# Gated attention and a maxout layer on one core: which output products are made of seven half products, and where five loads of v stand

## The chip, the core and the metric

The kernel runs on one core of one Trainium2 chip. The metric is the time of one execution in microseconds of the device; several executions are timed and the median is taken. A profile is one execution of its own, recorded by the hardware profiler.

## The reference

Eight sequences of 3072 tokens pass through an attention without softmax, gated by u, and then through a maxout layer with an output product.

```python
# u, v: (8, 3072, 256); z: (8, 3072, 64)
scores = (1.0 / S) * np.matmul(z, z.transpose(0, 2, 1))
attn = np.maximum(scores, 0.0) ** 2
x = u * np.matmul(attn, v)               # (24576, 256) in rows
# w1, w2: (256, 1024); w_out: (1024, 256)
g = np.maximum(x @ w1, x @ w2)
out = g @ w_out
```

The kernel computes max(x w1, x w2) as relu(x (w1 - w2)) + x w2, so that the output is g w_out + x (w2 w_out), where g now means the rectified part.

## The kernel before, in words

The work is cut into 48 steps: a step n is one group s of 512 tokens (n = 6 b + s, s from 0 to 5) of one sequence b. In its step each group gets its attention products with all 24 blocks of 128 keys. Scores between two groups are made once: the tile of a group and a later one is rectified, squared, and also transposed by a DMA on SP's queue (the tiles named aT), so that the later step can read it.

The attention product of a step (`add_sums`, line 613) is itself a Strassen-like product in the form of Winograd with seven half products: VectorE makes sums of tiles (es) and of v (lf, `add_fold`, line 366), TensorE makes the products X and Y into the two accumulator banks acc, and `add_ends` (line 750) puts them together: a copy e by ScalarE, sums by VectorE, and a multiplication with the transposed u that gives xT.

Three steps later on TensorE the second layer follows (`add_second`, line 1065): four products of xT with w1 - w2 (the pieces "da" and "db"), each rectified into g, and then the output product of g with w_out plus xT with W2o. The output product of step n stands at the beginning of step n + 3 (`put_o`, line 1276). It has two forms:

- The plain form (`parts`, line 1184): for four blocks of 128 tokens, ten products each with 256 moving columns, as two halves of 64 rows that run side by side, 80 matmuls in all. Two pairs of PSUM banks hold the result, and ScalarE (or VectorE) copies each pair out (`oc`).
- Seven half products (`add_seven`, line 924): g and w_out are cut into quarters, VectorE makes four sums of quarters of g (G1 to G4, tiles gs and g_sb), TensorE makes 72 matmuls of 128 rows and 128 moving columns, ScalarE copies twice (oc0, oc1), and VectorE adds the pieces into the output tile o_sb in six sums (oA to oF).

Which form a step takes is set in line 241: by s in `SEVEN` (line 54) and n below 46. Before the change that is s = 0, 1, 2 and 4, 31 steps in all.

Halves of 64 rows that write the same bank are ordered by a mark: a one-column memset on POOL that waits for the newest matmul (`mark`, line 94), and for which a later matmul waits. POOL also issues the loads of u, v and z (`load`, line 107); such a load waits for the newest matmul at its place in TensorE's order. So a load can stand ahead of a mark in POOL's queue. `quiet` (line 1477) moves a load's place to the next job of a list of jobs (`QUIET`, line 1473) behind which no mark is due soon. `at_step(b, s, us)` names the job of TensorE that by the plan's costs begins so many microseconds after step s of sequence b.

The tiles of v for a sequence are six loads of 512 tokens, in the order of `v_order` (line 319): groups 1, 2, 3, 4, 5, 0 for every sequence but the first. Two loads share a tile, and six such tiles exist (line 65): two sequences' worth. The sums lf of a pair can begin when both its loads have landed.

TensorE's order is written out by the planner from the list of jobs. The order on VectorE, ScalarE, SP and POOL comes from a list scheduler with costs and due times (`find_orders`, line 1748), which also chooses the engine of rectifiers and squares (lines 1787 and 1793); it is run 24 times, and the best plan is kept. Both change when the costs of jobs or the places of loads change.

Of the kernel before, what the change touches and what calls it, by code (L numbers as in the profile page):

```python
# [11 lines left out]
def kernel(  # L12
# [38 lines left out]
    NDIAG = 2  # L51
    PLAIN = 3
    NA, NT, WIDE = 16, 18, 19
    SEVEN = (0, 1, 2, 4)
    SEVEN_FROM, SEVEN_TO = 0, 46
    SPARE_D = (46, 2)
    DIAG_LAG = 8700, 6700
# [49 lines left out]
    def load(timed=False, **kw):  # L107
        dma = pin(nc.gpsimd.dma_start(**kw))
        if timed:
            tc.add_manual_dep(  # L110
                dma.ins,
                newest[0].name,
                mybir.DependencyInfo(mybir.DependencyClass.Sync, mybir.DependencyReason.DATA),
                reason="timed load",
            )
# [108 lines left out]
    def job(key, ways, fn, deps=(), new=None, uses=(), after=(), lag=100):  # L224
        assert key not in jobs, key
        jobs[key] = Job(key, ways, fn, deps, new, uses, after, lag)

    def buf(pool, key, make):
        bufs[pool, key] = Buf(make)
        order.setdefault(pool, []).append(key)  # L230
# [4 lines left out]
    class Step:  # L235
        def __init__(self, n, b, s):
# [3 lines left out]
            self.parted = 0 < n < B * NG - LAG + 1  # L240
            self.seven = s in SEVEN and SEVEN_FROM <= n < SEVEN_TO
            self.count = [0] * KD
# [76 lines left out]
    def v_order(b):  # L319
        return [1, 2, 3, 4, 5, 0] if b else list(range(NG))  # L320

    def v_pair(b, g):

        return divmod(v_order(b).index(g), 2)

    def v_key(b, g):
        return ("v", (b, v_pair(b, g)[0]))

    def v_tile(b, g):
        return tile_of(*v_key(b, g))[:, v_pair(b, g)[1]]  # L330
# [13 lines left out]
    def add_v(b, g, at):  # L344
        first = v_pair(b, g)[1] == 0
        if first:
            buf(*v_key(b, g), lambda: vpool.tile([P, 2, G, D], bf16, name="v_sb"))

        def fetch(_):
            load(  # L350
                timed=at is not None,
                out=v_tile(b, g),
                in_=v[b].rearrange("(p t) d -> p t d", p=P)[:, ds(g * G, G), :],
            )

        job(
            ("v", b, g),
            {"POOL": 1300},
            fetch,
            new=v_key(b, g) if first else None,  # L360
            uses=[v_key(b, g)],
            after=list(at or ()) + ([] if first else [("v", b, v_order(b)[v_order(b).index(g) - 1])]),
            lag=8000,
        )
# [1099 lines left out]
    def pe_job_at(ns):  # L1464
        found = [key for key, at in zip(pe_order, pe_at) if at >= ns]
        return [found[0]] if found else [pe_order[-1]]


    def at_step(b, s, us):
        return pe_job_at(starts[NG * b + s] + us * 1000)  # L1470
# [6 lines left out]
    def quiet(at):  # L1477
        i = pe_order.index(at[0])
        if pe_at[i] < starts[LAG]:
            return at  # L1480
        found = [key for key in pe_order[i:] if key in QUIET]
        return found[:1] or at
# [32 lines left out]
    def add_z(b, at, turn_at):  # L1515
        def fetch(_):
            load(
                timed=True,
                out=z_sb_0[:, 1 : 1 + NSB, :],
                in_=z[b].rearrange("(p t) d -> p t d", p=P),  # L1520
            )

        def turn_z(_):
            seqs[b].zT = make_zT(z_sb_0)

        job(("z", b), {"POOL": 1800}, fetch, after=at, lag=7500)
        job(("zT", b), {"SP": 3500}, turn_z, deps=[("z", b)], after=turn_at, lag=3500)
# [3 lines left out]
    for n in range(len(steps)):  # L1531
        b, s = steps[n].b, steps[n].s
# [5 lines left out]
    for b in range(1, B):  # L1538
        if b == 1:
            z_at, zT_at = (2, 6), (3, 2)  # L1540
            v_at = [(0, 8), (3, 12), (3, 16), (4, 4), (4, 8), (5, 4)]
        else:
            z_at, zT_at = (2, 9), (3, 4)
            v_at = [(3, 11), (3, 16), (4, 5), (4, 12), (5, 2), (5, 6)]
        add_z(b, quiet(at_step(b - 1, *z_at)), at_step(b - 1, *zT_at))
        for g, at in zip(v_order(b), v_at):
            add_v(b, g, quiet(at_step(b - 1, *at)))

    W2, W2T = ("T", "w2"), ("T", "w2T")
    bufs[W2] = Buf(lambda tag: widepool.tile([P, KD, Dff], bf16, name="w2_sb", tag=tag))  # L1550
# [421 lines left out]
```

## Time and profile before

| What | Value |
|---|---|
| timed runs | 907.89, 915.62 and 908.76 us; median 908.76 |
| the profiled execution | 907.76 us |
| its span | 905.9 us |
| TensorE (PE) | 898.3 us busy, 13565 matmuls |
| weight loads (PEld) | 673.1 us |
| VectorE (DVE) | 811.1 us |
| ScalarE (ACT) | 687.6 us |
| GpSimd (POOL) | 89.0 us |
| granted clock of TensorE | 1.00 |

The span runs from the first to the last instruction of the program; the time of the execution holds a little more at both ends. Busy times are unions of an engine's instructions. Matmuls are pipelined, so that one of 256 columns is shown with 0.27 us while the next starts after 0.11; times of products are therefore taken here from start to start.

Durations that the prediction uses, as mean time of one instruction from the groups of the profile:

| Instruction | Count | Mean |
|---|---|---|
| DVE gs<-g_sb, 128x1024 | 62 | 689 ns |
| DVE gs<-g_sb,gs, 128x1024 | 31 | 688 ns |
| DVE g_sb<-g_sb, 128x1024 | 31 | 690 ns |
| DVE o_sb<-o_sb,s_ps, 128x256 | 93 | 417 ns |
| DVE ot<-o_sb,s_ps, 128x256 | 31 | 416 ns |
| DVE o_sb<-o_sb,s_ps, 128x512 | 31 | 681 ns |
| DVE o_sb<-o_sb,ot, 128x512 | 31 | 683 ns |
| DVE a_sb<-a_sb (a square), 128x1024 | 160 | 689 ns |
| DVE a_sb<-a_sb (a square), 128x256 | 8 | 284 ns |
| ACT a_sb<-a_sb (a square), 128x1024 | 133 | 1068 ns |
| ACT a_sb<-a_sb (a square), 128x256 | 37 | 435 ns |
| ACT o_sb<-s_ps, 128x512 | 63 | 593 ns |
| ACT o_sb<-s_ps, 128x256 | 35 | 376 ns |
| POOL load of v | 48 | 534 ns |
| POOL mark | 302 | 102 ns |
| from a load's issue to its landing | 48 | 5.3 us (median) |

### The profile page before, as it was taken

The numbers are of one execution on the slowest core, as the hardware profiler recorded it, in microseconds if no ns is written. First come the engines' busy times: TensorE is split into PE (matmuls) and PEld (weight loads), VectorE is DVE, ScalarE is ACT, GpSimd is POOL, SyncE is SP. The second block draws the span as 40 slices with busy tenths as digits, with TensorE's granted clock in tenths as the row PEclk, the third lists the DMA queues.
The fourth block names the chain that finished last, engine by engine and source line by source line (L and its number), as shares of the span: only waits on it lengthen the run. The fifth ranks groups of instructions, "written<-read, shape, count | busy, mean of one in ns | idle before, by whom it ended". The sixth has DMA issues, their size and how long they took to land.

```text
span 905.9 us, 31722 instructions
## 1 busy us (share of the span) xinstructions
PE 898.3 (99%) x13565; PEld 673.1 (74%) x13565; DVE 811.1 (90%) x1594; ACT 687.6 (76%) x852; POOL 89.0 (10%) x417
## 2 busy tenths in 40 slices
PE   9999999999999999999999999999999999999998
PEld 3367777777777877778777877778777777777785
DVE  6888999899998999899998999989999899998970
ACT  8867987678877788677896688965989569885625
POOL 3101000111011110001100011000200011000000
PEclk9999999999999999999999999999999999999999
DMA  9999999999999999999999999999899989997711
GB/s 158 182 182 187 195 181 132 195 135 167 188 144 193 158 150 169 175 182 167 147 165 192 173 154 143 176 196 162 145 171 161 200 139 166 177 151 149 123 60 72
DMA packets 382911, 146.32 MB, mean 162 GB/s; under 512 B 361264, under 2 KB 362928, under 8 KB 382768
## 3 DMA queue, kind: packets, MB, share of 16 engines
q1 hardware_dynamic: 366208, 114.54, 74.4%
q0 software_dynamic: 16560, 29.74, 22.5%
q8 instruction: 106, 1.74, 0.8%
q14 instruction: 37, 0.30, 0.1%
HBM read 59.77 MB, written 25.17 MB: 94 GB/s over the span
## 4 chain that ended last, share of the span: by engine, by line
PE 94%; ACT 2%; DVE 2%; issue 1%; DMA 0%; POOL 0%; POOLq 0%; DVEq 0%
PE acc L87 48%; PE s_ps L87 46%; ACT a_sb L276 1%; DVE es L290 1%; ACT a_held L276 0%; ACT a_sb L282 0%; DVE es L293 0%; DVE o_sb L290 0%; DMA o_sb<-in_z_dram 0%; ACT o_sb L287 0%; DVE e L290 0%; DVE aT L293 0%; DVE xT L297 0%; DVE ot L290 0%; DVE a_sb L293 0%
## 5 line engine op out<-in xcount | busy, mean ns | idle before, releaser
L87 PEld LDWEIGHTS <-v_sb 64*128 64x128 bf16 (+1 forms) x4464 | 311.4, 94 | 80.1 <-POOL mark_sb L95 14.5
L276 ACT ACTIVATE a_sb<-s_ps 128x1024 bf16<-128x1024 f32 x337 | 300.7, 946 | 88.5 <-PE s_ps L87 87.3
L87 PEld LDWEIGHTS <-lf 64*128 64x128 bf16 x3240 | 251.4, 94 | 44.8 <-POOL mark_sb L95 15.5
L87 PE MATMUL acc<-es,v_sb 64*128 64x256 bf16 x2160 | 277.9, 269 | 0.4 <-DVE es L290 0.4
L87 PE MATMUL acc<-es,lf 64*128 64x256 bf16 x1080 | 247.8, 269 | 0.1
L87 PE MATMUL acc<-a_sb,lf 64*128 64x256 bf16 x1224 | 226.9, 269 | 0.0
L276 ACT ACTIVATE g_sb<-s_ps 128x1024 bf16<-128x1024 f32 x187 | 186.0, 1028 | 9.7 <-PE s_ps L87 8.4
L87 PE MATMUL s_ps<-xT,w_sb 64*128 64x512 bf16 (+1 forms) x1484 | 189.4, 377 | 1.2 <-ACT g_sb L276 0.9
L87 PE MATMUL acc<-aT,lf 64*128 64x256 bf16 x936 | 174.3, 269 | 0.0
L282 ACT ACTIVATE a_sb<-a_sb 128x1024 bf16<-128x1024 bf16 (+1 forms) x170 | 153.1, 930 | 0.8
L87 PE MATMUL acc<-a_sb,v_sb 64*128 64x256 bf16 (+1 forms) x1352 | 140.8, 280 | 0.1
L284 DVE TENSOR_TENSOR a_sb<-a_sb 128x1024 bf16<-128x1024 bf16 (+1 forms) x168 | 111.0, 669 | 29.4 <-ACT a_sb L276 27.9
L290 DVE TENSOR_TENSOR e<-e,acc 128x512 f32<-128x512 f32 (+1 forms) x225 | 125.8, 576 | 9.3 <-PE acc L87 5.2
L87 PEld LDWEIGHTS <-w_sb 64*128 64x128 bf16 (+1 forms) x1488 | 69.1, 94 | 72.1 <-POOL mark_sb L95 29.7
L87 PEld LDWEIGHTS <-g_sb 64*128 64x128 bf16 (+1 forms) x2016 | 107.8, 96 | 13.0 <-issue 7.0
L87 PE MATMUL s_ps<-zT 64*128 64x512 bf16 (+2 forms) x774 | 115.6, 333 | 0.5 <-DVE zT L131 0.3
L290 DVE TENSOR_TENSOR es<-aT 128x1536 bf16<-128x1536 bf16 (+1 forms) x117 | 105.9, 931 | 0.9 <-PE acc L87 0.2
L287 ACT COPY o_sb<-s_ps 128x256 f32<-128x256 f32 (+1 forms) x98 | 47.1, 516 | 72.7 <-PE s_ps L87 72.7
L95 POOL MEMSET mark_sb<- 128x1 bf16 x302 | 30.7, 102 | 719.3 <-PE acc L87 477.2
L87 PE MATMUL s_ps<-w_out_sb,g_sb 64*128 64x256 bf16 (+1 forms) x1520 | 99.4, 253 | 0.0
L87 PE MATMUL acc<-aT,v_sb 64*128 64x256 bf16 x936 | 84.8, 270 | 0.1
L293 DVE TENSOR_TENSOR es<-a_sb 128x512 bf16<-128x512 bf16 x198 | 79.9, 418 | 3.8 <-PE acc L87 3.3
(68 smaller groups left out, 878.8 us busy)
## 6 DMA issues: line engine op xcount, KB each, us to landing
out_dram<-o_sb SPq DMA_DIRECT2D x47, 512.0 KB, 5.3
v_sb<-in_v_dram POOLq DMA_DIRECT2D x48, 256.0 KB, 5.3
u_sb<-in_u_dram POOLq DMA_DIRECT2D x48, 256.0 KB, 5.1
aT<-a_sb SPq DMA_TRANSPOSE x230, 4.4
z_sb<-in_z_dram POOLq DMA_DIRECT2D x7, 384.0 KB, 7.2
w_sb<-in_moe_w_dram POOLq DMA_DIRECT2D x2, 512.0 KB, 7.3
uT<-u_sb SPq DMA_TRANSPOSE x48, 4.7
a_sb<-a_sb SPq DMA_TRANSPOSE x45, 4.4
```

What stands on the lines that cost most here:

```text
L87: newest[0] = pin(nc.tensor.matmul(*args, **kw)).ins
L95: ins = pin(nc.gpsimd.memset(mark_sb, 0.0)).ins
L276: pin(nc.scalar.activation(out_ap, in_ap, AF.Relu))
L282: pin(nc.scalar.activation(ap, ap, AF.Square))
L284: pin(nc.vector.tensor_mul(ap, ap, ap))
L287: pin(nc.scalar.copy(out_ap, in_ap) if eng == "ACT" else nc.vector.tensor_copy(out_ap, in_ap))
L290: pin(nc.vector.tensor_add(*args))
L293: pin(nc.vector.tensor_sub(*args))
```

## The change

Two things are edited. The set of steps whose output is made of seven half products loses s = 4: steps 4, 10, 16, 22, 28, 34 and 40 take the plain form (step 46 took it already), which leaves 24 steps of 31. And the six loads of v of the second sequence (b = 1) get other places, of which the first is the same; they are no longer moved by `quiet`. Loads of later sequences keep their rule.

```diff
-    SEVEN = (0, 1, 2, 4)
+    SEVEN = (0, 1, 2)
     SEVEN_FROM, SEVEN_TO = 0, 46
...
         if b == 1:
             z_at, zT_at = (2, 6), (3, 2)
-            v_at = [(0, 8), (3, 12), (3, 16), (4, 4), (4, 8), (5, 4)]
+            v_at = [(0, 8), (3, 9), (3, 14), (4, 2), (5, 2), (5, 8)]
...
         for g, at in zip(v_order(b), v_at):
-            add_v(b, g, quiet(at_step(b - 1, *at)))
+            add_v(b, g, quiet(at_step(b - 1, *at)) if b > 1 else at_step(b - 1, *at))
```

In the built program TensorE's order is the same job for job; 7 x 72 matmuls of 128 rows become 7 x 80 of 64 rows. VectorE has 1548 instructions instead of 1596: 70 of the seven steps are gone, and 22 squares (15 of 128x1024, 7 of 128x256) have come over from ScalarE. ScalarE has 22 fewer: those squares, while two copies for each of the seven steps stay, as two of 128x512 in place of one of 128x256 and one of 128x512. POOL has 14 more marks. The loads of v wait for other matmuls, and the order of squares, sums, transposes and stores in the first sequence is rearranged; the store of step 2, for one, stands ten places later on SP's queue.

## Prediction

> **What bounds the kernel now.** I read four views, from the whole to the place. First the page's busy times with its chain of work, and TensorE's own waits:
>
> ```profile
> span 905.9 us, 31722 instructions
> ...
> PE 898.3 (99%) x13565; PEld 673.1 (74%) x13565; DVE 811.1 (90%) x1594; ACT 687.6 (76%) x852; POOL 89.0 (10%) x417
> ...
> PE 94%; ACT 2%; DVE 2%; issue 1%; DMA 0%; POOL 0%; POOLq 0%; DVEq 0%
> ```
>
> ```profile
> PE s_ps L87 <- ACT g_sb L276: 0.9, 1, 0.9
> PE acc L87 <- DVE es L290: 0.4, 1, 0.4
> PE s_ps L87 <- POOL mark_sb L95: 0.3, 1, 0.3
> ```
>
> TensorE is the bound: 99% busy, 94% of the chain. Its waits after the start are three, 1.6 us together. The windows say where:
>
> ```profile
> 80.00:100.00 20.00, 19.47 (x304) 14.74 (x300) 18.84 (x41) 17.92 (x24) 2.19 (x9) 1.00 1.09 191
> 100.00:120.00 20.00, 18.94 (x290) 14.72 (x291) 19.42 (x42) 16.26 (x19) 1.87 (x10) 1.00 1.07 178
> 225.00:335.00 110.00, 110.00 (x1748) 84.92 (x1744) 102.80 (x204) 86.18 (x107) 10.84 (x53) 1.00 1.01 168
> ```
>
> The columns are the stretch, its length, then PE, PEld, DVE, ACT, POOL busy, granted clock, DMA share, GB/s. A whole sequence (225 to 335) shows TensorE busy 110.00 of 110.00 us: no relief of another engine can gain anything there. Only 80 to 120, inside the first sequence, has holes, and there VectorE is busy 94 and 97%.
>
> Then the timeline of TensorE at both forms of the output product, the seven half products of step 4 and the plain one of step 5:
>
> ```profile
> 132.10 0.27 PE L87 MATMUL acc<-a_sb,lf 64*128 64x256 bf16 x1
> 132.31 1.07 PE L87 MATMUL s_ps<-w_out_sb,g_sb 128*128 128x128 bf16 x16
> ...
> 136.43 0.39 PE L87 MATMUL acc<-a_sb,v_sb 64*128 64x256 bf16 x4
> ```
>
> ```profile
> 150.67 0.27 PE L87 MATMUL acc<-es,lf 64*128 64x256 bf16 x1
> 150.77 1.04 PE L87 MATMUL s_ps<-w_out_sb,g_sb 64*128 64x256 bf16 x16
> ...
> 155.14 0.38 PE L87 MATMUL acc<-aT,v_sb 64*128 64x256 bf16 x4
> ```
>
> From the last product before to the first one after, the seven half products take 136.43 - 132.10 = 4.33 us, the plain product 155.14 - 150.67 = 4.47 us. The switch into full rows (0.21 us instead of 0.10 from the start before it) is inside the 4.33.
>
> **The change part by part.** *Products.* Steps 4, 10, ... 40 are seven steps (46 is plain already). Each goes from 4.33 to 4.47: 7 x 0.14 = +1.0 us, all of it on the path. TensorE's order is otherwise the same, job for job.
>
> The page "TensorE: Matmul & The Clock Gate", section "Back-to-back issue gap", in the Trainium skill gives about 81 ns per matmul in a sustained stream of 128 columns. By that the 72 matmuls would cost 5.8 us and their removal would gain 7 x (5.83 - 4.47) = 9.5 us. This trace disagrees: eight of them start every 0.45 us (133.43, 133.88, 134.33), 56 ns each.
>
> *VectorE and ScalarE.* In each of the seven steps VectorE loses three gs sums and one g_sb sum (4 x 0.69), four of 256 columns (4 x 0.42) and two of 512 (2 x 0.68): 5.8 us, 40.5 in all. ScalarE loses copies of 0.38 and 0.59 and gets two of 0.59. The list scheduler uses the room: 22 squares more stand on VectorE (15 x 0.69 + 7 x 0.28 = 12.3 us) and fewer on ScalarE. VectorE should be busy near 783 us, ScalarE near 670. On the path: nothing, since TensorE does not wait from 120 us on.
>
> POOL gets 14 more marks of 0.10 us. Each of a plain product's two marks has 1.09 us of products ahead of its reader, as in steps 3 and 5; if that cover were gone, one mark costs TensorE about 0.3 us, as in the waits above.
>
> *The five loads of v that move.* The first load stays at 21 us. The others were issued at 68.35, 69.22, 82.75, 86.81 and 101.19; now they wait for the matmuls that started at 60.89, 65.46, 76.86, 95.94 and 102.48, and POOL follows such a start by about 0.5 us. One is put directly ahead of a mark that is read soon:
>
> ```profile
> 66.40 0.10 POOL L95 MEMSET mark_sb<- 128x1 bf16 x1 [0.79 <-PE s_ps L87]
> ```
>
> ```profile
> 214.82 0.53 POOL L108 DMA_DIRECT2D u_sb<-in_u_dram  x1 [0.45 <-PE acc L87]
> 215.51 0.10 POOL L95 MEMSET mark_sb<- 128x1 bf16 x1 [0.16 <-PE s_ps L87]
> ```
>
> The load would run from 65.96 to 66.49 and the mark follow 0.16 later, at 66.65 instead of 66.40. The matmul behind it (start near 66.56) has no slack to speak of, and TensorE's queue is behind that. Bounds 0 and 0.53 (the whole load); I take 0.25, the row of 214.82. The load at 102.98 ends at 103.51, before its mark is due (103.73): nothing. The 61 and 66 us loads now fall beside two transposes of z on SP's queue (58.02 to 62.66) and of aT (66.01 on). POOL's queue moved 29.74 MB in 22.5% of 905.9 us, so a 0.26 MB load is 1.8 us of the 16 engines. A transpose that is that much later costs TensorE 0 to 1.8 us; I take 0, as no wait of TensorE or VectorE after the start ends in a transpose. The second pair of v is complete earlier (77 instead of 83 us). The third is complete by 102.98 + 5.3 = 108.3, and its first sum ran at 112.09: 3.8 us of cover; without it VectorE would stand still for the remainder.
>
> *The holes of the first sequence.* The reordered queues reach them. TensorE's start times show five: 0.29 at 81.0 (the o_sb sums of step 1), 0.57 at 86.7 (an es sum), 0.23 at 103.2, 1.02 at 104.8 and 0.30 at 106.5: 2.4 us. The largest:
>
> ```profile
> 104.91 1.98 ACT L276 ACTIVATE g_sb<-s_ps 128x1024 bf16<-128x1024 f32 x2
> ...
> 106.02 0.61 PE L87 MATMUL s_ps<-xT,w_sb 64*128 64x512 bf16 x4 [0.85 <-ACT g_sb L276]
> ```
>
> TensorE waits for a bank that ScalarE's rectifier (104.91) reads late, behind its copy of e at 104.44. In the changed order two squares (1.07 each) no longer stand ahead of that copy. Likewise one square (0.69) and two sums (2 x 0.42) leave VectorE's queue ahead of the sums behind the holes at 81.0 and 86.7. So each single wait should go. What is late next is VectorE: from 77 to 125 us it idles only about 2.3 us in pieces, and its work there stays the same (a square of 0.69 and an o_sb sum of 0.68 leave the stretch, two squares come in). If TensorE comes 2.4 us earlier, VectorE must lose all its idle time to follow. Bounds: 0 and -2.4. I take half, -1.2.
>
> *Sum*, against the profiled execution (span 905.9, its time 907.76): +1.0 + 0.25 - 1.2 = 0.0. The three timed runs have the median 908.76, 1.0 above that execution; the forecast is 908.8.
>
> **The rivals.** (1) The holes stay: VectorE, at 94 to 97%, makes TensorE wait at other sums. For it: those rows. Against: the largest hole is ScalarE's. Then +1.0 + 0.25 = +1.25: 910.0.
>
> (2) Slower, by ScalarE behind the plain product: its second copy (0.59) can start only when the product ends, at 136.7 instead of inside it, and the rectifiers queue behind it. For it: rectifiers feed scores that need a bank. Against: ScalarE idles 1.81 us at that place (134.5 + 0.86 to 137.19), and steps 3 and 5 do the same without a wait. It decides when that copy, which can end at 137.3, ends after the score that takes its pair of banks: the scores behind the product start at 136.77, 137.64 and 138.41, there are three pairs, and the third score needs this one, so the slack is 1.1 us. Price: one copy per sequence, 7 x 0.59 = 4.2, to both, 8.3: 913.0 to 917.1, and 918.3 on top of rival 1.
>
> (3) A moved load delays transposes that are read at once: 1.8 us once gives 910.6, twice 912.4. For it: in the first 120 us the DMA engines are as full as anywhere (share 1.07 to 1.09 in the rows above). Against: no engine waits for a transpose there.
>
> (4) The half products cost more than they seem, so that leaving them gains. As a mechanism of rows: if each matmul had to wait for its own weights (98 ns mean for the 128x128 loads), 72 would take 7.06 us, and 7 x (7.06 - 4.47) = 18 us would be gained: 890.6. Starts 56 ns apart exclude it. The Trainium skill's 81 ns above would lie between.
>
> That the change does less than it says is excluded: seven steps change form and five loads move in the built order.
>
> **How the numbers follow.** Chances: forecast 0.70 (its own range 907.4, all holes gone, to 909.5), rival 1 0.17, rival 2 0.08, rival 3 0.04, rival 4 0.01. The first two fill 907.4 to 910.0; the runs of before scatter by about 0.9 around their median apart from one, and one late transpose adds 1.8, so the range is 906.5 to 911.5. About 1% (9 us) is what a measurement of this kernel can tell from no change. Only rival 4 is faster than that: 0.01. Slower by over 1%, past 917.8, needs rival 2 at its upper end on top of rival 1, or several late transposes: 0.03. Within 1%: 0.96.
>
> **What would show it.** Right: windows of 110 us from 225 on with TensorE busy throughout, each sequence 0.14 us longer; output pieces of 4.47 us in step 4; VectorE near 783 us busy; the mark near 66 us late by some 0.25; TensorE's wait at 104.8 gone and VectorE's share there near 100%. Wrong: a wait of TensorE for ScalarE or VectorE that recurs in each sequence behind the plain product of step 4, or waits in the first sequence that end in a transpose.

## The result, and the profile after

| | before | after |
|---|---|---|
| median | 909.15 us (16 executions, 907.72 to 916.27) | 916.02 us (16 executions, 913.15 to 922.32) |
| profiled execution, span | 907.76, 905.9 us | 920.87, 919.0 us |

The ratio is 1.0078 (95% interval 1.0058 to 1.0098), 7 us slower; forecast were 908.8 us and a range of 906.5 to 911.5. The ratio leaves out executions more than 1.5% above the fastest of their kernel. The executions of one kernel spread over several microseconds here, and the spread turns out to be the subject: of the kernel before 8 of 16 stay at or below 909.0 us, of the changed one none.

Page of the profile after, the lines that answer to the first ones of before:

```profile
span 919.0 us, 31781 instructions
...
PE 905.8 (99%) x13621; PEld 677.8 (74%) x13621; DVE 787.5 (86%) x1546; ACT 676.9 (74%) x830; POOL 90.8 (10%) x431
...
PE 92%; DMA 3%; DVE 2%; ACT 2%; issue 1%; POOL 0%; POOLq 0%; DVEq 0%
```

VectorE and ScalarE have become idler, about as forecast (783 and 670 us). New is DMA with 3% of the chain, where it had 0%. TensorE's waits (us in total, times, longest):

```profile
PE acc L87 <- DMA aT<-a_sb: 3.8, 2, 1.9
PE s_ps L87 <- issue: 2.8, 1, 2.8
PE zeros L87 <- DVE blank L166: 1.2, 1, 1.2
PE acc L87 <- DVE e L290: 0.6, 1, 0.6
PE s_ps L87 <- POOL mark_sb L95: 0.3, 1, 0.3
```

The wait for ScalarE's g_sb (0.9) is gone. In its place TensorE waits twice for aT, a transposed tile, and stops once for 2.8 us for which the list names no releaser ("issue"; the last section tells what goes with it). Two windows of before that the prediction does not show, and then those of after (same columns):

```profile
40.00:60.00 20.00, 20.00 (x162) 10.61 (x161) 17.06 (x34) 14.95 (x18) 2.11 (x4) 1.00 1.21 175
60.00:80.00 20.00, 20.00 (x328) 16.45 (x327) 15.96 (x34) 11.96 (x17) 2.09 (x8) 1.00 1.09 178
```

```profile
40.00:60.00 20.00, 18.05 (x122) 8.55 (x121) 15.45 (x29) 15.23 (x18) 2.02 (x3) 1.00 1.27 138
60.00:80.00 20.00, 19.66 (x283) 15.47 (x280) 13.68 (x29) 11.42 (x16) 2.21 (x9) 0.91 1.23 143
80.00:100.00 20.00, 16.91 (x219) 13.19 (x216) 14.01 (x31) 10.32 (x16) 1.67 (x8) 0.83 1.16 153
100.00:120.00 20.00, 18.17 (x282) 13.84 (x282) 17.57 (x36) 15.68 (x20) 2.10 (x8) 1.00 1.16 188
...
235.00:345.00 110.00, 110.00 (x1750) 84.80 (x1747) 99.04 (x196) 84.33 (x105) 11.18 (x55) 1.00 1.03 165
```

The span is 13.1 us longer, and all but some 3 us of that come ahead of 125 us. TensorE stands still for 2 us already between 40 and 60, where it had none idle (20.00 of 20.00 before), and from 60 to 100 the granted clock is 0.91 and 0.83. The starts of the output products in the trace, in us, count it (the two experiments are told below):

| output product of step | before | after | w1 cut | loads spread |
|---|---|---|---|---|
| 0 | 58.03 | 60.87 | 58.25 | 58.17 |
| 1 | 74.00 | 78.73 | 74.49 | 74.41 |
| 3 | 113.41 | 123.76 | 111.87 | 111.79 |
| 4 | 132.31 | 143.44 | 130.67 | 130.59 |
| a later sequence, start to start | 110.12 | 110.41 | 110.41 | 110.42 |

The first stop, in the timeline of TensorE of the changed kernel:

```profile
57.55 0.38 PE L87 MATMUL acc<-aT,v_sb 64*128 64x256 bf16 x4
59.88 0.28 PE L87 MATMUL acc<-aT,lf 64*128 64x256 bf16 x2 [1.95 <-DMA aT<-a_sb]
59.99 0.27 PE L87 MATMUL acc<-a_sb,v_sb 64*128 64x256 bf16 x1
60.45 0.38 PE L87 MATMUL acc<-a_sb,v_sb 64*128 64x256 bf16 x3 [0.20 <-DMA a_sb<-a_sb]
60.87 1.07 PE L87 MATMUL s_ps<-w_out_sb,g_sb 128*128 128x128 bf16 x16
```

The aT that step 3 wants landed at 59.84 us. The first load at a new place is issued at 65.87. So what made this transpose late came earlier.

Two of the stops are paid twice. Windows of 2 us show it for the first in their PEclk column, the third from the end:

```profile
58.00:60.00 2.00, 0.12 (x3) 0.11 (x3) 0.40 (x2) 0.00 (x0) 0.00 (x0) 1.00 1.13 166
60.00:62.00 2.00, 1.80 (x27) 1.34 (x24) 2.00 (x6) 0.00 (x0) 0.10 (x1) 0.95 1.29 268
62.00:64.00 2.00, 2.00 (x22) 2.00 (x20) 1.57 (x4) 0.00 (x0) 0.00 (x0) 0.50 1.13 57
64.00:66.00 2.00, 2.00 (x28) 2.00 (x27) 0.76 (x2) 0.86 (x2) 0.13 (x1) 0.69 1.24 265
66.00:68.00 2.00, 2.00 (x39) 1.75 (x38) 1.21 (x3) 0.62 (x1) 0.93 (x2) 1.00 1.09 207
```

After the pause the clock is at one half from 61.81 for 3.41 us. The stop of 3.0 us at 80.1 is followed by 6.83 us of half clock, in which eight products of the output start every 0.85 us (84.25, 85.10, 85.96) instead of every 0.45. The output product of step 1 takes 9.70 us for 4.33, the stop included. By starts, the stops are 2.1 and 0.35 us (57.7 and 60.0), 3.0 (80.1) and 2.0 (109.7); with half of 3.41 + 6.83 us that makes 12.6 us. The product of step 3 is 11.97 us later than in the kernel with its loads spread, which has no such stop, so 0.6 us of this sum are too much; against the kernel before, whose holes that kernel closes, it is 10.35 us late. The Trainium skill, "TensorE: Matmul & The Clock Gate", section "What's actually happening", gives the half clock after an idle window of about 3.4 us, in windows of 3413 ns. The lengths 3.41 and 6.83 us agree; the pause ahead of the first was shorter, 2.1 and 0.35 us, and the one of 2.0 us at 109.7 brought no half clock.

### The profile page after: what moved, and what is told of

Read it like the earlier page. It is cut to its first block, busy times and chain, and to the rows that moved or that the text cites. A ratio compares the mean times of both kernels' runs of the same rounds, so it can differ in the third digit from the quotient of the medians.

```text
span 919.0 us, 31781 instructions
## 1 busy us (share of the span) xinstructions
PE 905.8 (99%) x13621; PEld 677.8 (74%) x13621; DVE 787.5 (86%) x1546; ACT 676.9 (74%) x830; POOL 90.8 (10%) x431
## 4 chain that ended last, share of the span: by engine, by line
PE 92%; DMA 3%; DVE 2%; ACT 2%; issue 1%; POOL 0%; POOLq 0%; DVEq 0%
PE acc L87 46%; PE s_ps L87 45%; DMA a_sb<-a_sb 1%; DMA v_sb<-in_v_dram 1%; ACT a_sb L276 1%; DMA aT<-a_sb 1%; DVE es L290 1%; ACT a_held L276 0%; PE zeros L87 0%; DVE e L290 0%; DVE es L293 0%; DVE a_sb L293 0%; PE tpz_c L130 0%; DVE lf L293 0%; DVE xT L297 0%
## 5 line engine op out<-in xcount | busy, mean ns | idle before, releaser
L87 PEld LDWEIGHTS <-v_sb 64*128 64x128 bf16 (+1 forms) x4464 | 307.4, 94 | 79.5 <-POOL mark_sb L95 14.4
L276 ACT ACTIVATE a_sb<-s_ps 128x1024 bf16<-128x1024 f32 x337 | 301.3, 944 | 84.8 <-PE s_ps L87 83.1
L87 PEld LDWEIGHTS <-lf 64*128 64x128 bf16 x3240 | 246.6, 94 | 50.6 <-POOL mark_sb L95 15.5
L284 DVE TENSOR_TENSOR a_sb<-a_sb 128x1024 bf16<-128x1024 bf16 (+1 forms) x190 | 122.5, 656 | 50.2 <-ACT a_sb L276 48.6
L282 ACT ACTIVATE a_sb<-a_sb 128x1024 bf16<-128x1024 bf16 (+1 forms) x148 | 135.4, 933 | 1.2
L87 PEld LDWEIGHTS <-g_sb 64*128 64x128 bf16 (+1 forms) x2240 | 117.7, 96 | 17.1 <-issue 8.4
L287 ACT COPY o_sb<-s_ps 128x256 f32<-128x256 f32 (+1 forms) x98 | 49.2, 530 | 98.8 <-PE s_ps L87 98.8
L87 PE MATMUL s_ps<-w_out_sb,g_sb 64*128 64x256 bf16 (+1 forms) x1856 | 121.0, 259 | 0.0
```

The costliest lines, as they stand in the source:

```text
L87: newest[0] = pin(nc.tensor.matmul(*args, **kw)).ins
L276: pin(nc.scalar.activation(out_ap, in_ap, AF.Relu))
L282: pin(nc.scalar.activation(ap, ap, AF.Square))
L284: pin(nc.vector.tensor_mul(ap, ap, ap))
L287: pin(nc.scalar.copy(out_ap, in_ap) if eng == "ACT" else nc.vector.tensor_copy(out_ap, in_ap))
```

## Experiments

All were timed in 5 rounds, those of one group beside one another on one chip, with runs of the kernel before between them. A transpose is counted by its place on SP's queue; the sixth turns block 14 of step 1. In the tables, "loads alone" is the kernel with the moved loads and the old products. "Landing" is the time from a DMA's start on its queue to its last semaphore event.

**Which half of the change.** The seven products alone (`SEVEN = (0, 1, 2)`, old places of loads), the moved loads alone (old `SEVEN`, new `v_at`), and the two kernels themselves again:

> Only the products change: s = 4 takes the plain form, the loads of v stay where they were. The queues are then those of before, job for job, up to about 126 us. Theory 1 (the loss is made in the first sequence, where the moved loads and the queues planned around them make transposes late): about 1 to 2 us slower than before, from 7 x 0.14 us of products and a little per sequence; no wait for a transpose before 120 us. Theory 2 (the plain product of step 4 rearranges VectorE and ScalarE and with them the transposes): most of the 6.9 us, 5 or more. Theory 3 (chance: DMA in the first 100 us is slow in some executions of any kernel): like theory 1, with single runs 5 us slower.

> Only the loads of v of the second sequence move; four of six steps keep seven half products. Theory 1: 4 to 6 us slower than before, with transposes that land 10 us or more after their issue, TensorE waiting for aT before 60 us and again near 110 us, and whole sequences of 110.12 us from 225 us on. Theory 2: within 1.5 us of before. Theory 3: within 1.5 us of before in most runs.

> The kernel before once more, for a second profile. Theories 1 and 2: output products of steps 0 to 3 start at 58.0, 74.0, 93.1 and 113.4 us again, within 0.5 us. Theory 3: these starts scatter by several us from profile to profile, as the timed runs between 907.7 and 916.3 do.

> The kernel after once more, for a second profile. Theories 1 and 2: the same places lose time as in its first profile (near 58, 80 and 110 us), with a granted clock under 1.0 only where TensorE stood still for some us; 913 to 918 us. Theory 3: other places, and a time anywhere from 909 to 922 us.

| | median | lowest | at or below 909.0 | ratio |
|---|---|---|---|---|
| products alone | 909.82 | 909.40 | 0 of 12 (7 at or below 910.0) | 1.0010 [0.9986, 1.0035] |
| loads alone | 915.16 | 909.88 | 0 of 12 | 1.0037 [1.0004, 1.0069] |
| before again | 908.98 | 907.43 | 6 of 12 | 1.0002 [0.9978, 1.0025] |
| after again | 915.62 | 913.31 | 0 of 11 | 1.0070 [1.0039, 1.0100] |
| shared before | 909.74 | 907.69 | 16 of 34 | |

The loads carry the loss; the products cost about 1.7 us by the lowest times (909.4 against 907.7). A comparison of the planned orders tells why the loads act so early: with their new places the list scheduler puts ScalarE's rectifier and VectorE's square of pair 16 of step 1 ahead of those of pair 14. In a listing of instructions both read alike, so the swap does not show there. SP's sixth transpose is then issued at 27.58 us, behind the load of u (27.14) and 0.1 us ahead of w1's (27.68), where it was issued at 26.76, ahead of both (26.87 and 27.41).

**Order, or loads and addresses.** The swap was put back in the changed kernel, made in the kernel before, and put back with the moved loads alone; a fourth kernel puts back another difference, SP's order near 47 us. `swap` exchanges two jobs in the finished plan:

```diff
+    swap(("relu", 1, 14), ("relu", 1, 16))
+    swap(("square", 1, 14), ("square", 1, 16))
```

```diff
+    swap(("turn", 0, 16), ("turn", 2, 16))
+    swap(("turn", 0, 18), ("turn", 2, 18))
```

> The changed kernel, with one thing put back: in step 1 ScalarE's relu and VectorE's square of pair 14 come ahead of those of pair 16 again, as in the kernel before; everything else is the changed kernel's, its tile slots, its later order of SP and its loads too. Theory A (the swap makes SP issue the transpose of pair 14 about 0.9 us later, behind the u load and beside the w1 load; it lands some 4 us late, the transposes behind it too, and TensorE waits 2 to 4.5 us for an aT at 57 us): the first output product starts at about 58.0 us as in the kernel before, no stop for aT stays, and the time is that of the kernel before less some 2.0 us of holes between the first and the fourth output product (56.2 us in the changed kernel, 58.3 before) plus seven times 0.29 us for the later sequences: 907 to 910 us, 0.4 us below to 1 us above the kernel before. Rival B (the loads of v or the tile slots that the plan hands out slow the transfers): the first output product still starts at 61 to 64 us, and the time stays at 913 to 917 us. Rival C (SP's later order, step 2's turned blocks ahead of step 0's): the start at 58.0 us holds only if no transfer before 52 us is late; a stop then comes later, and the time lies between, 911 to 914 us.

> The kernel before, with only that swap of step 1 made in it: relu and square of pair 16 ahead of those of pair 14. No load is moved and no product changed. Theory A: the transposes from the sixth on land 4 us late, TensorE waits 2 to 4.5 us for an aT at about 57 us, the first output product starts at 61 to 64 us, and the time is 911 to 916 us, 3 to 7 us above the kernel before. Rivals B and C: first output product at 58.0 us, 907.5 to 909.5 us, the same as the kernel before.

> The kernel before with the moved loads alone (seven half products in four steps of six, as before) and the order of step 1 put back. Theory A: first output product at 58.0 us, fourth 56.2 us later instead of 58.3, later sequences 110.12 us as before: 2.0 us below the kernel before, 905.5 to 907.5 us, the fastest of all. Rival B: 912 to 916 us, as the moved loads alone gave. Rival C: 908 to 912 us.

> The changed kernel with SP's order near 47 us put back instead (step 0's held blocks 16 and 18 turned ahead of step 2's blocks 16 and 18, as in the kernel before); the swap in step 1 stays. Theory A: the sixth transpose is late as in the changed kernel, TensorE stops for an aT at 57 us, first output product at 61 to 64 us, 912 to 917 us. Rival C: first output product at 58.0 us and 907 to 910 us.

| | median | lowest | at or below 909.0 | ratio |
|---|---|---|---|---|
| after, step 1 put back | 910.36 | 907.68 | 6 of 12 | 1.0000 [0.9966, 1.0034] |
| before, with the swap | 914.11 | 908.26 | 1 of 12 | 1.0027 [0.9998, 1.0057] |
| loads alone, step 1 put back | 913.30 | 906.19 | 2 of 12 | 1.0015 [0.9978, 1.0051] |
| after, SP's order put back | 917.19 | 913.35 | 0 of 12 | 1.0062 [1.0028, 1.0096] |
| shared before | 910.97 | 907.46 | 13 of 35 | |

Rival C is out: with SP's order put back no execution is in time. The swap is a cause, but theory A as expected is too simple: with step 1 put back half of the executions are at 907.7 to 908.4 us, and the other half still late. And in the loads alone with step 1 put back, where theory A expected 905.5 to 907.5 us, what rival B expected came: a median of 913.30 us, 2 of 12 in time, and in the profile the first output product at 61.46 us. So the swap is not all by which the moved loads, or what the plan changes with them, make executions late, as far as 12 executions tell. In the profiled execution of the changed kernel with step 1 put back (914.94 us) the sixth transpose is issued at 26.69, as before, and yet lands after 12.9 us. The kernel before has such executions too, and with the swap in it only one of 12 is in time, though the interval of its ratio still touches 1, and in its profile the sixth transpose took 14.7 us, but the first output product came at 59.2 us instead of the expected 61 to 64 and the stops from 97 us on. So the swap only tips a balance: what holds the transposes up is there in both kernels.

The products alone have late executions of their own, 4 of 12 at 914.5 to 916.0 us. In the profiled one (914.47) the sixth and the twelfth transpose are in time (7.0 and 9.2 us), and so are the output products of steps 0 to 2. Three later ones, issued at 82.5 to 87.9 us beside the loads of v at their old places (83.1 and 87.1), land after 10.3, 14.8 and 13.5 us, and TensorE waits for them near 100 us:

```profile
PE acc L87 <- DMA aT<-a_sb: 3.3, 2, 2.3
```

**What holds them up.** Views of DMA from 26 to 41 us, before and after. The first line is SP's queue, all of it transposes; the last number of a line with a tile is us to landing:

```profile
q1 hardware_dynamic: 7579, 1.89, 71.9%
...
w_sb<-in_moe_w_dram POOLq DMA_DIRECT2D x1, 512.0 KB, 8.4
...
aT<-a_sb SPq DMA_TRANSPOSE x5, 4.2
w2T_sb<-w_sb SPq DMA_TRANSPOSE x1, 6.5
```

```profile
q1 hardware_dynamic: 5564, 1.39, 66.8%
...
w_sb<-in_moe_w_dram POOLq DMA_DIRECT2D x1, 512.0 KB, 10.9
...
aT<-a_sb SPq DMA_TRANSPOSE x4, 8.8
w2T_sb<-w_sb SPq DMA_TRANSPOSE x1, 9.9
```

In the same 15 us a quarter less is transposed, and everything that runs beside w1's load lands late. Then w_out's load (40.7 us) meets what is left over. So one eighth of w1's load was left, one eighth of w_out's, and w1 was moved, in these kernels:

```diff
-            load(timed=True, out=tile_sb(), in_=source.rearrange(rows, p=P))
+            if tile_sb() is w1_sb:
+                pin(nc.gpsimd.memset(w1_sb[:, :, P:], 0.0))
+                load(timed=True, out=w1_sb[:, :, :P], in_=source.rearrange(rows, p=P)[:, :, :P])
```

```diff
+    behind(("w1",), ("plain", 1, 12))
```

> The changed kernel with one eighth of the load of w1 (128x2x128 instead of 128x2x1024; the rest of the tile is set to zero by POOL, so the shared weights are computed from other data). Nothing else is changed, the swap of step 1 and the moved loads stay. Theory A, as it now stands: an execution is late when the transposes that SP issues from 26.7 us on run beside the load of w1 at 27.5 us; each then takes 11 to 15 us from issue to landing instead of 7, and the lateness reaches TensorE at 57 to 118 us. With most of that load gone the sixth transpose lands after 7 us or less, the first output product starts at about 58 us, and most executions take 907.5 to 909 us (the changed kernel: none of 27 under 913). Rival D (lateness comes from the sum of all traffic up to 140 us, whichever load it is): most executions stay at 912 to 917 us.

> The changed kernel with step 1's order put back and the load of w1 issued some 5 us later, behind the plain product of block 12 of step 1 instead of ahead of that of block 4. Theory A: the transposes issued at 26.7 to 28 us land before w1's packets come; the late executions (6 of 12 without this) become rare, median 907.5 to 908.5 us. Rival D: as many late executions as before, median 908 to 914 us. A third outcome, w1 now beside the transposes of w2 and of the blocks behind it at 32 to 40 us, would show as transposes 8 to 12 taking over 9 us and a median of 912 us or more.

> The changed kernel with the load of w1 issued some 5 us later and the swap of step 1 left in. Theory A: the swap costs nothing without w1 beside the sixth transpose; most executions at 907.5 to 909 us. If the swap itself makes the transposes late (the order, not the company), 912 to 917 us as in the changed kernel.

> The kernel before with the load of w1 issued some 5 us later, nothing else. Theory A: its late executions (over 909 us; 19 of 35 in the last comparison) become rare, median 907.5 to 908.2 us. Rival D: no difference in their share.

(By count 22 of those 35 executions were over 909 us, not 19.)

| | median | lowest | at or below 909.0 | ratio |
|---|---|---|---|---|
| after, w1 cut | 907.96 | 907.66 | 11 of 12 | 0.9967 [0.9935, 0.9999] |
| after, step 1 put back, w1 5 us later | 914.49 | 909.87 | 0 of 12 | 1.0031 [0.9996, 1.0066] |
| after, w1 5 us later | 913.37 | 909.29 | 0 of 12 | 1.0020 [0.9988, 1.0052] |
| before, w1 5 us later | 911.43 | 908.28 | 1 of 12 | 0.9980 [0.9948, 1.0012] |
| shared before | 910.71 | 907.66 | 12 of 35 | |

With the swap and the moved loads still in it, the changed kernel without most of w1's load loses its lateness in 11 of 12 executions. (What is left of the load is issued at 29.1 us instead of 27.7, behind the memset; a load that is only moved later, below, does not help.) Its view of DMA, same 15 us:

```profile
q1 hardware_dynamic: 7486, 1.87, 65.7%
...
aT<-a_sb SPq DMA_TRANSPOSE x5, 3.4
w_sb<-in_moe_w_dram POOLq DMA_DIRECT2D x1, 64.0 KB, 5.4
w2T_sb<-w_sb SPq DMA_TRANSPOSE x1, 4.3
```

Rival D (any traffic) expected 912 to 917 us here. This alone does not exclude it, as the cut takes traffic away as well; the kernels with spread loads, below, do, as nothing is left out there. Moving the load 5 us later is the third outcome named: it now runs beside transposes 8 to 11 (7 to 10 us each in the changed kernel, 13 to 17 in the kernel before), and the twelfth lands after 11 to 17 us. In the kernel before TensorE then also waits 2.4 us for w_out's load itself.

**The second link, and a place for both loads.** Next, w1 cut in the kernel before, w_out cut in the changed one (`w_out_sb[:, :1, :]` loaded, the rest zeroed), and w1 at the place of the load of v(1,1), with that load put to 66 us:

```diff
+    behind(("w1",), ("v", 1, 1))
+    behind(("v", 1, 1), ("o", 0, 1))
```

> The kernel before with one eighth of the load of w1 (the rest of the tile set to zero by POOL; the shared weights are computed from other data), all else unchanged. Theory A: its own late executions are made by the same load: 907.4 to 908.3 us in at least 10 of 12 executions, where the kernel before has about half of its executions over 909. Rival E (they come from something else, such as the chip's other traffic): about half stay over 909 us. Beside the changed kernel with the same cut (907.96 us) it also gives the price of the change without late transposes: by the starts of the output products 0.2 us, as the holes give back 1.9 us and seven sequences cost 0.29 us each.

> The changed kernel with one eighth of the load of w_out (the rest of the tile set to zero by POOL, so the output is computed from other data), w1 whole and all else unchanged. If w_out's load at 40.7 us is the second link (transposes late from w1 are still under way when it begins and are held up again, 15 to 17 us each), the sixth to the ninth transpose stay late (10 to 11 us) but the twelfth lands by 54 us instead of 60, the first output product starts at 58 to 59 us, and the time is 908 to 910 us. If w1's lateness alone reaches TensorE, 912 to 917 us.

> The changed kernel with step 1's order put back, the load of w1 at the place of the load of v(1,1) (21.7 us instead of 27.4), and that load of v, wanted only by the second sequence, at 66 us just ahead of v(1,2). Nothing is left out. Theory A: w1 is landed by about 30 us, the transposes from the sixth on have half a megabyte less beside them, late executions become rare, and the median is 907.5 to 908.5 us. If w1 now holds up the fourth and the fifth transpose instead (over 9 us each), the chain begins earlier and the time is 911 to 916 us.

> The same two loads at these other places and step 1's order put back, with seven half products in four steps of six as in the kernel before (the moved loads alone). Theory A: the same as the kernel beside it less seven times 0.29 us: 905.8 to 906.8 us, below the kernel before. If the fourth and fifth transpose are held up instead: 909 to 914 us.

| | median | lowest | at or below 909.0 | ratio |
|---|---|---|---|---|
| before, w1 cut | 909.17 | 907.74 | 6 of 12 | 0.9966 [0.9937, 0.9996] |
| after, w_out cut | 907.89 | 907.35 | 8 of 12 | 0.9969 [0.9928, 1.0009] |
| after, step 1 put back, w1 at 22 us | 910.38 | 908.09 | 3 of 12 | 0.9988 [0.9953, 1.0023] |
| loads alone, the same | 910.76 | 907.14 | 5 of 12 | 0.9995 [0.9962, 1.0028] |
| shared before | 911.78 | 907.54 | 12 of 35 | |

Either cut alone frees most executions of the changed kernel, so most of its lateness needs both loads: w1's makes transposes late, w_out's catches the late ones. Not all of it: without most of w_out's load 3 of 12 still take 914.9 to 919.4 us. The expected 10 of 12 in the kernel before with w1 cut were 6, though none was above 912.3 us; w_out's load still held its transposes up in some (the twelfth to fifteenth took 7.7 to 12.5 us in its profile). The earlier place of w1 was not enough either. In the profile of the changed kernel with it (916.90 us) the first output product comes in time, at 58.49 us, and the late transposes are the 20th to 22nd (11.9, 13.5 and 10.1 us), beside the loads of v and u at 62 to 67 us.

Last, with those places, w_out's load was put between the transposes of step 1 and those of step 2, at 33 us. Nothing is left out:

```diff
+    behind(("wo",), ("plain", 1, 14))
```

> The changed kernel with step 1's order put back, w1's load at 22 us, the load of v(1,1) at 66 us, and w_out's load at about 33 us instead of 41, between the transposes of step 1 and those of step 2. Nothing is left out. Theory A (two large loads in a row beside the transposes of 27 to 46 us make the lateness): the twelfth transpose, at 41 us, lands in 7 us or less instead of 10, nothing reaches TensorE, and most executions take 907.5 to 908.5 us. If w_out's load now delays the eighth to eleventh transpose past 44 us, the u and z loads at 42 and 47 us take its part, and most executions stay at 910 to 915 us.

> The same places of the loads and step 1's order put back, with seven half products in four steps of six as in the kernel before. Theory A: most executions take 905.8 to 907.0 us, below the kernel before (fast ones 907.5 to 908.2), as the holes are closed and the later sequences take 110.12 us. Otherwise as the kernel beside it less 2 us: 908 to 913 us.

| | median | range | at or below 909.0 | ratio |
|---|---|---|---|---|
| changed kernel, loads spread | 908.14 | 907.82 to 910.26 | 9 of 12 | 0.9978 [0.9952, 1.0003] |
| loads spread, old products | 906.12 | 905.81 to 909.24 | 11 of 12 | 0.9963 [0.9945, 0.9980] |
| shared before | 908.78 | 907.51 to 918.95 | 12 of 23 | |

The twelfth transpose lands after 5.2 and 6.1 us instead of 15.7 in the changed kernel and 10.0 before. The first row is the changed kernel nearly without late transposes: 0.7 us under the forecast. The second is faster than both kernels. Windows of the first:

```profile
40.00:60.00 20.00, 20.00 (x160) 10.50 (x159) 17.06 (x34) 15.10 (x18) 1.19 (x3) 1.00 1.19 188
60.00:80.00 20.00, 19.86 (x323) 15.87 (x322) 15.76 (x32) 12.78 (x18) 3.17 (x10) 1.00 1.21 179
80.00:100.00 20.00, 19.73 (x312) 15.11 (x307) 19.27 (x42) 16.85 (x23) 1.68 (x8) 1.00 1.14 196
100.00:120.00 20.00, 20.00 (x316) 15.17 (x315) 19.42 (x42) 16.75 (x20) 2.08 (x12) 1.00 1.20 175
```

After the start TensorE has no stop for a DMA left, and 100 to 120 is full where the kernel before had 18.94.

## Why the prediction was wrong, step by step

- **Products, +1.0: right.** Step 4's product takes 4.47 us in the changed kernel, each time.
- **The mark near 66 us, +0.25: right.** The space between two starts there is 0.52 us instead of 0.23, +0.29, in the changed kernel and with its loads spread.
- **Holes, −1.2: right in kind, too small.** With the loads spread and the old products, the products of steps 0 and 4 stand 72.52 us apart against 74.28. As the mark adds 0.29, that is 2.05 us of 2.4 closed; the bound was nearer than the middle. VectorE did lose idle time: with the loads spread in the changed kernel it idles 1.72 us between the products of steps 1 and 4, and 3.68 before. (From 77 to 125 us it idled 2.0 us before, not 2.3.)
- **VectorE and ScalarE off the path behind 120 us: nearly.** A sequence became 0.29 us longer, not 0.14. The other 0.15 lies between the output products of steps 0 and 1 of each (18.07 us for 17.92). The list scheduler put a sum of o_sb ahead of both multiplications into xT; it waits for ScalarE's copy, and all that stands behind it on VectorE with it. Timelines of VectorE at that place, before, and in the changed kernel with spread loads:

```profile
280.65 1.01 DVE L290 TENSOR_TENSOR e<-e,acc 128x256 f32<-128x256 f32 x2
281.58 0.68 DVE L297 SCALAR_TENSOR_TENSOR xT<-e,uT 128x512 bf16<-128x512 f32 x1
282.18 0.41 DVE L290 TENSOR_TENSOR o_sb<-o_sb,s_ps 128x256 f32<-128x256 f32 x1
```

```profile
279.76 1.01 DVE L290 TENSOR_TENSOR e<-e,acc 128x256 f32<-128x256 f32 x2
281.14 0.42 DVE L290 TENSOR_TENSOR o_sb<-o_sb,s_ps 128x256 f32<-128x256 f32 x1 [0.38 <-ACT o_sb L287]
281.48 1.29 DVE L297 SCALAR_TENSOR_TENSOR xT<-e,uT 128x512 bf16<-128x512 f32 x2
```

  Counted from the start of the output product, VectorE's later work ends some 0.4 us later. With it comes the last sum e that reads the accumulators (11.48 us instead of 11.08), and the first of the products acc<-es,lf, which by the profile waits for that sum, starts 0.17 us later (11.53 instead of 11.36). It is no wait in TensorE's list, since overlapping matmuls hide it; only starts show it. That this order is the reason is read from the timelines and was not run by itself. Seven times 0.29 us is the 2.0 us between the two last kernels (908.14 and 906.12). The parts add up: 1.0 + 0.29 - 2.05 + 7 x 0.15 is +0.3 us, and the spans of the changed kernel with spread loads and of the kernel before are 906.2 and 905.9 us.
- **Late transposes, "I take 0, as no wait of TensorE or VectorE after the start ends in a transpose": this step failed.** By medians it was worth +7.9 us (916.02 against 908.14), with the half clock and, in some executions, the late read of instructions that the last section tells of. The second profile of the changed kernel (913.31 us) shows it alone: one wait for aT of 3.6 us by starts, and 3.41 us of half clock behind it, make the output product of step 3 come 5.3 us later than with the loads spread (117.06 and 111.79), and the execution is 5.2 us longer (908.07). The profile of before was one of the executions in which all transposes came in time; that no wait ended in one there says nothing of the margin. The sign was in the three times shown, 915.62 beside 907.89 and 908.76, and was set aside as scatter. The prediction's own sign of being wrong, a wait in the first sequence that ends in a transpose, is what came. The price was bounded by one load's 1.8 us on the moved loads. But the two loads whose removal or new place brings most executions in time, w1's and w_out's, are not moved by the change; it reached them through the planner, which swapped two pairs 40 us ahead of the first load that has a new place.
- **The moved loads have a part of their own, which no run separates.** Among the transposes issued between 58 and 76 us, where two of the moved loads now stand, the slowest takes 10 to 15 us in 10 of the 14 profiles with the moved loads, and at most 8.4 us in the six with the old places. In three of those six the slow ones are issued at 80 to 92 us instead (11.6, 12.3 and 14.8 us), where two of them stood.
- **The clock** was not in the sum: in the first profile of the changed kernel the pauses of 2.1 and 0.35 us and of 3.0 us were followed by 3.41 and 6.83 us at half clock, which cost some 1.7 and 3.4 us more.
- **Rivals.** 1 (holes stay) and 2 (ScalarE behind the plain product) did not come; no wait that recurs behind step 4 exists. 4 is excluded: the products alone cost time. 3 named the right end, TensorE waiting for a transpose, at a quarter of the size, and with 0.04. The place and the loads that it named are the smaller part, as far as the runs tell: the changed kernel with most of w1's load left out has the moved loads still, and is in time in 11 of 12.

## What to carry to other kernels

A wait that is absent from one profile is not a margin: where timed executions of one kernel differ by several microseconds, find which transfer comes late in the long ones before costing a change at nothing. A scheduler that fills queues by cost can be moved far ahead of the edit, and two orders can read alike line by line; compare the planned jobs, not the instructions. In this kernel large loads belong between groups of transposes that are waited for, not beside them.

## What the runs showed of the hardware

- The same transposes land after 3 to 7 us or after 10 to 17, by the loads that run beside them. From 40 to 61 us, with the same three loads beside it, SP's queue moved these packets before and after (the last number is the share of 16 engines' time):

```profile
q1 hardware_dynamic: 9252, 2.30, 75.5%
```

```profile
q1 hardware_dynamic: 7239, 1.80, 84.1%
```

  That is 27 ns of engine time for a packet, and 39. The load of z took 7.6 us there before and 13.1 after. The Trainium skill, "DMA: Bandwidth & Descriptors", section "Queues, rings and completion order", says that an engine takes turns between its queues packet by packet. The direction agrees.
- SP issued its ninth transpose 0.65 to 0.85 us after the sixth had landed in all eight profiles in which the sixth took over 10 us (39.32 after 38.52 in the changed kernel). The only thing that its instruction waits for, a load of u, had landed long before; SP is shown in the eighth transpose until then, for 7.02 us instead of 4.44 before. Lateness so passes down the queue.
- The stop of 3.0 us at 80.1 us is a late read of instructions, as far as the profiles tell. In every one of the 20 profiles a read of 16 KB on the instruction queue stands near the output product of step 1. In 15 it ends 0.17 us or more ahead of that product's start, and nothing stops. In five it ends after the start, and then TensorE stops at the same matmul, the 26th of the product, and goes on 1.49 to 1.60 us after the read has ended: in the changed kernel the read ran from 79.64 to 81.53 us and TensorE went on at 83.12. These five all have transposes of 10 to 15 us shortly before, so that the read seems late for the same reason, but this is argued. With the half clock behind it this stop is about half of what the first profile of the changed kernel lost by the product of step 3 (5.8 of 11.97 us).
- Which execution of the same program is late was not settled. Shown are two loads without which most are in time, and places for them that do the same with nothing left out.
